# Right-side SBUF tiles moved by 96 bytes, and the second products of a feed-forward block issued output by output

## The chip, the cores and the metric

The kernel runs on one core of one Trainium2 chip. The metric is device time in microseconds (us), the median of several runs. TensorE (PE) multiplies, VectorE (DVE), ScalarE (ACT) and GpSimd (POOL) do the element-wise work, SyncE (SP) issues nearly all transfers.

## What is computed

Causal attention with a decay bias (4 batches, 8 heads, 576 positions, head size 64), then two feed-forward blocks over all 4 x 576 = 2304 tokens, with 64-bit weights, the rest float32:

```python
scores = q @ k.T / 8 + min(-(cum_i - cum_j), 0), causal; attn = softmax(scores); x = attn @ v
h = x @ w_in;  x = max(0.01 * h, h) @ w_out                              # block 0
h = x @ w_in2; out = (max(h, 0) + log1p(exp(-|h|))) @ w_out2             # block 1
```

with `w_in` 512 x 2048 and `w_out` 2048 x 512.

## The kernel before

Every float32 matrix is split into a high part of float32r type and a low part that holds the rest (`xh`/`xl`, `wih`/`wil`, `woh`/`wol`, `gh`/`gl`), and a product is three passes: high with high, high with low, low with high. The first 276 us are attention, with some of block 0 run in between (class `Fill`). The loop from line 685 on does the rest of block 0 and all of block 1.

The 2048 hidden features are cut into 16 tiles of 128, four tiles (`G = 4`) to a weight group, so each block has four groups. The tokens are cut into chunks of 512, 512, 256, 512 and 512 (for the first group of block 0, two chunks of 288). One **step** is one hidden tile `f` of one chunk of one group:

- `h_mm` (line 137) makes the hidden tile: 12 matmuls into one PSUM bank, `xh`, `xl`, `xh` moving, weights `wih`, `wih`, `wil`, four times.
- `act1` (line 599) applies the activation. In block 1 that is a chain over engines: ACT makes `e` and `l`, POOL makes `t` (line 619), DVE makes `gf` (624), ACT makes `gh` (149), POOL makes `gl` (150), one step behind the other.
- `out_mm` (line 632) runs three steps later (`LAG = 3`). It adds the hidden tile's share to the outputs: four outputs in block 0 (rows of the model size, `gh`/`gl` moving, weights `woh`/`wol`), and `N // 128` outputs in block 1 (token tiles, `woh`/`wol` moving 512 columns, `gh`/`gl` as weights). Each output has one PSUM bank (`ps_out`, five buffers) which collects all four steps of a chunk; at the fourth (`f == G - 1`) each output is added into `acc` by DVE (line 662; copied by ACT, line 660, in the first group), and in the last group of block 1 stored (line 665).

The order inside `out_mm` before: first, output by output, the two passes with `gh`; then, output by output, the pass with `gl`; then, after all of it, the sums. All instructions of an engine run in the order of the program; the two planned weight splits (`split_w`) put DVE, ACT and POOL work between the steps.

Pools with `side="right"` are stacked downwards from the end of SBUF. In the built program every tile on the left that TensorE reads (`xh` at byte 16,512 of each partition, `wih` at 90,240, `woh` at 106,624) starts at a multiple of 128, and every tile on the right (the loop's `gh` and `gl` from 212,960 to 227,296, `gf`, `t`, `e`, `l`, and the raw weights and `gh`/`gl` of `Fill`) starts 96 bytes behind one.

Of the kernel before, what the change touches and what calls it, by code (L numbers as in the profile page):

```python
# [9 lines left out]
F32 = mybir.dt.float32  # L10
# [7 lines left out]
P = 128  # L18
NEG = -8.0e9
G = 4  # L20
# [10 lines left out]
def attn_moe_moe(ctx, tc, q, k, v, s, w1i, w1o, w2i, w2o, out):  # L31
    nc = tc.nc
# [7 lines left out]
    NG = NF // G  # L40
# [9 lines left out]
    def pool(name, bufs=1, **kw):  # L50
        return tc.tile_pool(name=name, bufs=bufs, **kw)

    dram = ctx.enter_context(pool("dram", space=bass.MemoryType.DRAM))
    keep = ctx.enter_context(pool("keep"))


    xh = keep.tile([P, KD, NT], F32R, tag="xh", name="xh")
    xl = keep.tile([P, KD, NT], F32R, tag="xl", name="xl")
# [7 lines left out]
    def later(n, fn, *args):  # L66
        todo.setdefault(clock[0] + n, []).append((fn, args))
# [515 lines left out]
    def acc_tile(c, i):  # L583

        c0, N = c
        n = 512 // N
        return acc[:, i * n:(i + 1) * n, c0:c0 + N]
# [42 lines left out]
    outs = {}  # L630

    def out_mm(n):
        layer, g, c, _, _, f = steps[n]
        c0, N = c
        gh, gl = gs.pop(n)
        wh, wl = wt[layer, g * G + f, "o"]
        n_out = KD if layer == 0 else N // P

        for i in range(n_out):
            if f == 0:  # L640
                outs[i] = ps_o.tile([P, 512], F32, tag="o", name="ps_out")
        for low in range(2):
            for i in range(n_out):
                sl = slice(i * P, (i + 1) * P)
                if layer == 0:
                    ps, ops = outs[i][:, :N], ((wh[:, sl], gh), (wl[:, sl], gh), (wh[:, sl], gl))
                else:
                    ps, ops = outs[i], ((gh[:, sl], wh), (gh[:, sl], wl), (gl[:, sl], wh))
                for m, (a, b) in enumerate(ops):
                    if (m == 2) == low:  # L650
                        nc.tensor.matmul(ps, a, b, start=f == 0 and m == 0, stop=f == G - 1 and m == 2)  # L651
        if f < G - 1:
            return
        for i in range(n_out):
            if layer == 0:
                d, o = acc[:, i, c0:c0 + N], outs[i][:, :N]
            else:
                d, o = acc_tile(c, i), outs[i].rearrange("p (a x) -> p a x", x=N)
            if g == 0:
                nc.scalar.activation(d, o, AF.Copy)  # L660
            else:
                nc.vector.tensor_tensor(d, o, d, op=ALU.add)  # L662
            if layer == 1 and g == NG - 1:
                r = c0 + i * P
                nc.sync.dma_start(out[r:r + P, :].rearrange("p (a x) -> p a x", x=N), d)
        if layer == 0 and g == NG - 1:
            later(1, split_x, slice(c0, c0 + N))


# [1 line left out]
    start = {}  # L671
    for n, st in enumerate(steps):
        start.setdefault(st[:2], n)
    for gi, (layer, g) in enumerate(groups[1:]):
        a, z = start[groups[gi]], start[layer, g]
        when = [a + 2, a + 5, a + 8, a + 11, z - 3, z, z - 1, z + 2]
        for j, n in enumerate(when):
            if gi == 0 and j < 4:
                continue
            f, nm = divmod(j, 2)  # L680
# [4 lines left out]
    for n, (layer, g, c, is_first, is_last, f) in enumerate(steps):  # L685
        N = c[1]
        cols = slice(c[0], c[0] + N)
        ps = ps_h.tile([P, 512], F32, tag="h", name="ps_h")
        h_mm(ps[:, :N], layer, g * G + f, xh[:, :, cols], xl[:, :, cols])
        tick()  # L690
        act1(n, layer, N, ps)
        for fn, w in sorted(plan.pop(n, ()), key=lambda x: x[0] is load_w):
            fn(*w)
        if n >= LAG:
            out_mm(n - LAG)
    for n in range(len(steps) - LAG, len(steps)):
        tick()
        out_mm(n)
# [48 lines left out]
```

## Time and profile before

| what | before |
|---|---|
| median of 3 runs | 1022.04 us (1021.41 to 1022.06) |
| span of the profiled execution, first to last instruction | 1020.2 us |
| instructions | 15105 |
| PE busy | 992.0 us, 97% |
| POOL, ACT, DVE busy | 559.2, 536.8, 506.3 us |
| mean granted TensorE clock | 0.997 |

The profiled execution's own time is its span plus what lies around it: the median of the runs is 1.8 us above the span. Matmuls are pipelined, so a matmul's listed duration (some 0.39 us for 512 columns) overlaps the next one's; the pace is the distance from start to start, which the chain of waits (pieces of 12 matmuls) and the timeline show. On the timeline a piece "x4" is four instructions that follow each other, and a bracket names the idle time before an instruction and what ended it. Time stretches: attention to 276 us, block 0 to about 600 us, block 1 to the end.

### The profile page before, as it was taken

The numbers are of one execution on the slowest core, as the hardware profiler recorded it, in microseconds if no ns is written. First come the engines' busy times: TensorE is split into PE (matmuls) and PEld (weight loads), VectorE is DVE, ScalarE is ACT, GpSimd is POOL, SyncE is SP. The second block draws the span as 40 slices with busy tenths as digits, with TensorE's granted clock in tenths as the row PEclk, the third lists the DMA queues.
The fourth block names the chain that finished last, engine by engine and source line by source line (L and its number), as shares of the span: only waits on it lengthen the run. The fifth ranks groups of instructions, "written<-read, shape, count | busy, mean of one in ns | idle before, by whom it ended". The sixth has DMA issues, their size and how long they took to land.

```text
span 1020.2 us, 15105 instructions
## 1 busy us (share of the span) xinstructions
PE 992.0 (97%) x5498; PEld 812.4 (80%) x5498; DVE 506.3 (50%) x1133; ACT 536.8 (53%) x1152; POOL 559.2 (55%) x565
## 2 busy tenths in 40 slices
PE   7889999999999999999999998999999999999998
PEld 4667788888998888888888887888778877888886
DVE  6886665554021312321244158547575767576443
ACT  4877676656355333432444365666645554565452
POOL 6757455434156335533553356667766676667453
PEclk9999999999999999999999999999999999999999
DMA  5422333210252002100220021101210121010202
GB/s 172 135 97 67 113 106 101 93 59 25 73 205 76 22 1 83 63 21 1 83 62 22 16 68 41 42 2 45 80 42 1 42 82 42 1 42 21 83 22 83
DMA packets 38518, 62.04 MB, mean 61 GB/s; under 512 B 2932, under 2 KB 25972, under 8 KB 38444
## 3 DMA queue, kind: packets, MB, share of 16 engines
q1 hardware_dynamic: 38204, 60.74, 18.2%
q8 instruction: 44, 0.72, 0.3%
q10 hardware_dynamic: 240, 0.33, 0.1%
q14 instruction: 30, 0.25, 0.1%
HBM read 52.65 MB, written 8.40 MB: 60 GB/s over the span
## 4 chain that ended last, share of the span: by engine, by line
PE 73%; POOL 10%; DVE 8%; issue 6%; ACT 3%; DMA 0%; DVEq 0%; POOLq 0%; ACTq 0%
PE ps_h L143 30%; PE ps_out L651 27%; PE pt_v L354 4%; PE ps_o L539 4%; PE pt_s L262 4%; POOL t L619 3%; PE pt_t L323 3%; POOL gl L150 2%; POOL wm L120 2%; DVE wm L114 2%; PE pt_s L252 2%; ACT sc L295 1%; DVE wm L111 1%; DVE wm L117 1%; POOL wil L130 1%
## 5 line engine op out<-in xcount | busy, mean ns | idle before, releaser
L150 POOL TENSOR_TENSOR gl<-gf,gh 128x512 fp32r<-128x512 f32 (+2 forms) x148 | 178.3, 1206 | 258.9 <-ACT gh L149 243.4
L143 PE MATMUL ps_h<-xh,wih 128*128 128x512 f32 (+2 forms) x688 | 246.5, 358 | 1.1 <-ACT o L543 0.6
L143 PE MATMUL ps_h<-xl,wih 128*128 128x512 f32 (+2 forms) x688 | 244.7, 356 | 0.0
L143 PE MATMUL ps_h<-xh,wil 128*128 128x512 f32 (+2 forms) x688 | 243.9, 354 | 0.0
L143 PEld LDWEIGHTS ps_h<-xh,wih 128*128 128x128 f32 x688 | 129.4, 188 | 21.5 <-ACT o L543 0.8
L306 POOL TENSOR_SCALAR sc<-sc,st 128x512 f32<-128x512 f32 (+4 forms) x160 | 88.1, 562 | 103.8 <-DVE st L302 61.3
L143 PEld LDWEIGHTS ps_h<-xl,wih 128*128 128x128 f32 x688 | 129.4, 188 | 19.0
L143 PEld LDWEIGHTS ps_h<-xh,wil 128*128 128x128 f32 x688 | 129.4, 188 | 18.5
L662 DVE TENSOR_TENSOR acc<-ps_out,acc 128x512 f32<-128x512 f32 (+1 forms) x114 | 67.7, 655 | 129.1 <-PE ps_out L651 129.1
L149 ACT ACTIVATE gh<-gf 128x512 fp32r<-128x512 f32 (+2 forms) x148 | 85.3, 576 | 82.7 <-DVE gf L624 81.8
L605 ACT ACTIVATE gf<-ps_h 128x512 f32<-128x512 f32 (+2 forms) x68 | 36.7, 539 | 172.1 <-PE ps_h L143 168.2
L651 PE MATMUL ps_out<-woh,gh 128*128 128x512 f32 x288 | 116.2, 403 | 5.8 <-ACT gh L149 3.2
L624 DVE TENSOR_TENSOR gf<-gf,t 128x512 f32<-128x512 f32 (+1 forms) x80 | 56.0, 700 | 127.0 <-POOL t L619 127.0
L111 DVE TENSOR_SCALAR wm<-wm 128x512 f32<-128x512 f32 x64 | 42.1, 658 | 147.3 <-ACT wm L105 140.3
L651 PE MATMUL ps_out<-wol,gh 128*128 128x512 f32 x288 | 115.0, 399 | 0.0
L295 ACT ACTIVATE sc<-sc,st 128x512 f32<-128x512 f32 (+2 forms) x144 | 83.3, 581 | 42.9 <-DVE st L286 22.0
L120 POOL TENSOR_TENSOR wm<-wm,wt 128x512 int32<-128x512 int32 x64 | 88.1, 1377 | 28.0 <-DVE wm L117 28.0
L619 POOL TENSOR_TENSOR t<-e,t 128x512 f32<-128x512 f32 (+1 forms) x80 | 98.3, 1228 | 0.0
L651 PE MATMUL ps_out<-gh,woh 128*128 128x512 f32 (+2 forms) x272 | 97.1, 365 | 0.0
L651 PE MATMUL ps_out<-gh,wol 128*128 128x512 f32 (+2 forms) x272 | 96.6, 364 | 0.0
L281 DVE CUSTOM_DVE_ANT_0 sc<-pt_s,mask 128x512 f32<-128x512 f32 (+2 forms) x144 | 66.7, 480 | 57.2 <-PE pt_t L323 46.1
L651 PE MATMUL ps_out<-woh,gl 128*128 128x512 f32 x288 | 80.6, 397 | 1.2 <-POOL gl L150 1.1
(93 smaller groups left out, 1729.2 us busy)
## 6 DMA issues: line engine op xcount, KB each, us to landing
rawi<-in_moe_w_in SPq DMA_DIRECT2D x32, 512.0 KB
rawo<-in_moe_w_out SPq DMA_DIRECT2D x32, 512.0 KB
V<-in_v SPq DMA_DIRECT2D x16, 320.0 KB
Q<-in_q SPq DMA_DIRECT2D x15, 320.0 KB
K<-in_k SPq DMA_DIRECT2D x16, 288.0 KB
out<-acc SPq DMA_DIRECT2D x18, 256.0 KB
part<-o SPq DMA_DIRECT2D x24, 144.0 KB
acc<-part SPq DMA_DIRECT2D x6, 576.0 KB
```

The source lines that it names most:

```text
L111: nc.vector.tensor_scalar(mf, mf, D_MIN, D_MAX, op0=ALU.max, op1=ALU.min)
L120: nc.gpsimd.tensor_tensor(m, m, t, op=ALU.add)
L143: nc.tensor.matmul(ps, a, b, start=n == 0, stop=n == 3 * KD - 1)
L149: nc.scalar.activation(gh, gf, AF.Copy)
L150: nc.gpsimd.tensor_tensor(gl, gf, gh.bitcast(F32), op=ALU.subtract)
L281: nc.vector.tensor_tensor_reduce(out=self.sc[:, j, c], in0=self.ps[j][:, c], in1=m, scale=-scale, scalar=3.0e38, op0=ALU.add, op1=ALU.min, ...
L295: nc.scalar.activation(x, x, AF.Exp, scale=-1.0, bias=self.stat(0, e), accum_out=self.stat(1, e))
L306: nc.gpsimd.tensor_scalar(x, x, self.stat(2, e), 1.0, op0=ALU.mult, op1=ALU.mult)
L619: nc.gpsimd.tensor_tensor(t, e, t, op=ALU.subtract)
L624: nc.vector.tensor_tensor(gf, gf, t, op=ALU.add)
L651: nc.tensor.matmul(ps, a, b, start=f == 0 and m == 0, stop=f == G - 1 and m == 2)
L662: nc.vector.tensor_tensor(d, o, d, op=ALU.add)
```

## The change

A pool of 96 bytes per partition is opened first on the right side and keeps its place to the end, and `out_mm` is rewritten:

```diff
-
+    edge = ctx.enter_context(pool("edge", side="right"))
+    edge.tile([P, 24], F32, tag="edge", name="edge")
...
-        for low in range(2):
-            for i in range(n_out):
...
-                for m, (a, b) in enumerate(ops):
-                    if (m == 2) == low:
-                        nc.tensor.matmul(ps, a, b, start=f == 0 and m == 0, stop=f == G - 1 and m == 2)
-        if f < G - 1:
-            return
         for i in range(n_out):
+            sl = slice(i * P, (i + 1) * P)
...
+            for m, (a, b) in enumerate(ops):
+                nc.tensor.matmul(ps, a, b, start=f == 0 and m == 0, stop=f == G - 1 and m == 2)
+            if f < G - 1:
+                continue
             if layer == 0:
                 d, o = acc[:, i, c0:c0 + N], outs[i][:, :N]
```

Every right-side tile starts 96 bytes lower in the built program, `gh` and `gl` at 212,864 to 227,200: multiples of 128, as on the left. The left side stays. Nothing writes or reads the new tile.

Each output's three passes now stand together, and on the last step of a chunk its sum follows in the program. The number of instructions is the same on every engine, and their order differs on PE alone: the sums were already the next instructions of DVE (or ACT), and stay where they were; what they wait for on PE comes earlier.

PE, one step of block 0 in the middle of a chunk (`ps_out` numbers are PSUM tiles), before and with the change:

```order
L651 MATMUL ps_out_4876<-gh_4825,woh_4318 128x512 [waits Activation_49]
L651 MATMUL ps_out_4876<-gh_4825,wol_4320 128x512
L651 MATMUL ps_out_4877<-gh_4825,woh_4318 128x512
L651 MATMUL ps_out_4877<-gh_4825,wol_4320 128x512
L651 MATMUL ps_out_4878<-gh_4825,woh_4318 128x512
L651 MATMUL ps_out_4878<-gh_4825,wol_4320 128x512
L651 MATMUL ps_out_4879<-gh_4825,woh_4318 128x512
L651 MATMUL ps_out_4879<-gh_4825,wol_4320 128x512
L651 MATMUL ps_out_4876<-gl_4826,woh_4318 128x512 [waits Pool_49]
L651 MATMUL ps_out_4877<-gl_4826,woh_4318 128x512
L651 MATMUL ps_out_4878<-gl_4826,woh_4318 128x512
L651 MATMUL ps_out_4879<-gl_4826,woh_4318 128x512
```

```order
L650 MATMUL ps_out_4880<-gh_4829,woh_4322 128x512 [waits Activation_49]
L650 MATMUL ps_out_4880<-gh_4829,wol_4324 128x512
L650 MATMUL ps_out_4880<-gl_4830,woh_4322 128x512 [waits Pool_49]
L650 MATMUL ps_out_4881<-gh_4829,woh_4322 128x512
L650 MATMUL ps_out_4881<-gh_4829,wol_4324 128x512
L650 MATMUL ps_out_4881<-gl_4830,woh_4322 128x512
L650 MATMUL ps_out_4882<-gh_4829,woh_4322 128x512
L650 MATMUL ps_out_4882<-gh_4829,wol_4324 128x512
L650 MATMUL ps_out_4882<-gl_4830,woh_4322 128x512
L650 MATMUL ps_out_4883<-gh_4829,woh_4322 128x512
L650 MATMUL ps_out_4883<-gh_4829,wol_4324 128x512
L650 MATMUL ps_out_4883<-gl_4830,woh_4322 128x512
```

The wait for POOL's `gl` moves from the ninth matmul to the third, and the bank changes four times in a step where it changed eight times.

PE, the first step of the last chunk of block 1, where the banks must be free of the chunk before, before and with the change:

```order
L651 MATMUL ps_out_9754<-woh_8349,gh_9692 128x512 [waits PE_49,Activation_49]
L651 MATMUL ps_out_9754<-wol_8351,gh_9692 128x512
L651 MATMUL ps_out_9755<-woh_8349,gh_9692 128x512 [waits DVE_49]
L651 MATMUL ps_out_9755<-wol_8351,gh_9692 128x512
L651 MATMUL ps_out_9756<-woh_8349,gh_9692 128x512 [waits DVE_49]
L651 MATMUL ps_out_9756<-wol_8351,gh_9692 128x512
L651 MATMUL ps_out_9757<-woh_8349,gh_9692 128x512 [waits DVE_49]
L651 MATMUL ps_out_9757<-wol_8351,gh_9692 128x512
L651 MATMUL ps_out_9754<-woh_8349,gl_9693 128x512 [waits Pool_49]
```

```order
L650 MATMUL ps_out_9758<-woh_8353,gh_9696 128x512 [waits PE_49,Activation_49]
L650 MATMUL ps_out_9758<-wol_8355,gh_9696 128x512
L650 MATMUL ps_out_9758<-woh_8353,gl_9697 128x512 [waits Pool_49]
L650 MATMUL ps_out_9759<-woh_8353,gh_9696 128x512 [waits DVE_49]
L650 MATMUL ps_out_9759<-wol_8355,gh_9696 128x512
L650 MATMUL ps_out_9759<-woh_8353,gl_9697 128x512
L650 MATMUL ps_out_9760<-woh_8353,gh_9696 128x512 [waits DVE_49]
L650 MATMUL ps_out_9760<-wol_8355,gh_9696 128x512
L650 MATMUL ps_out_9760<-woh_8353,gl_9697 128x512
L650 MATMUL ps_out_9761<-woh_8353,gh_9696 128x512 [waits DVE_49]
```

The waits for DVE's sums of the chunk before move from the third, fifth and seventh matmul to the fourth, seventh and tenth.

## Rows read from the trace of the kernel before

**Rows 1.** The page, part 1: busy time of each engine, share, instructions.

```profile
PE 992.0 (97%) x5498; PEld 812.4 (80%) x5498; DVE 506.3 (50%) x1133; ACT 536.8 (53%) x1152; POOL 559.2 (55%) x565
```

**Rows 2.** The chain in order of time (start, us, what): 512 columns in block 0.

```profile
527.73 2.76 PE ps_h L143 x12
530.49 2.81 PE ps_out L651 x12
```

**Rows 3.** The same chain, block 1: 512 columns, and a step with two outputs.

```profile
906.53 2.73 PE ps_h L143 x12
909.26 2.81 PE ps_out L651 x12
...
973.23 1.40 PE ps_out L651 x6
```

**Rows 4.** Timeline of PE, block 1: one `h_mm`, its fourth matmul and its twelfth.

```profile
907.06 0.39 PE L143 MATMUL ps_h<-xh,wih 128*128 128x512 f32 x1
...
908.87 0.39 PE L143 MATMUL ps_h<-xh,wil 128*128 128x512 f32 x1
```

**Rows 5.** Timeline of PE, block 0: a step's first matmul, its four with gl, what follows.

```profile
469.02 0.40 PE L651 MATMUL ps_out<-gh,woh 128*128 128x512 f32 x1
...
470.90 1.10 PE L651 MATMUL ps_out<-gl,woh 128*128 128x512 f32 x4
471.83 0.40 PE L143 MATMUL ps_h<-xh,wih 128*128 128x512 f32 x1
```

**Rows 6.** Timeline of PE: a step of 256 columns in block 0, and what follows.

```profile
460.61 0.28 PE L651 MATMUL ps_out<-gh,woh 128*128 128x256 f32 x1
...
462.05 0.39 PE L143 MATMUL ps_h<-xh,wih 128*128 128x512 f32 x1
```

**Rows 7.** The chain in order of time: an `h_mm` of 256 columns in block 0.

```profile
543.09 1.44 PE ps_h L143 x12
```

**Rows 8.** Groups by line and form: first passes of block 0 and block 1.

```profile
L651 PE MATMUL ps_out<-woh,gh 128*128 128x512 f32 x288 | 116.2, 403 | 5.8 <-ACT gh L149 3.2 <-DVE acc L662 2.1 <-ACT acc L660 0.5
L651 PE MATMUL ps_out<-gh,woh 128*128 128x512 f32 x192 | 76.3, 398 | 0.0
```

**Rows 9.** Busy time by stretch: length, PE, PEld, DVE, ACT, POOL, granted clock, DMA.

```profile
697.00:766.00 69.00, 66.79 (x308) 53.77 (x307) 48.24 (x64) 40.38 (x75) 49.25 (x39) 1.00 0.14 46
800.00:867.00 67.00, 64.92 (x300) 52.40 (x299) 50.90 (x69) 36.90 (x67) 46.76 (x36) 1.00 0.15 48
```

**Rows 10.** Timeline, block 1, 761 to 763 us: a step with two outputs.

```profile
761.25 0.40 PE L651 MATMUL ps_out<-woh,gh 128*128 128x512 f32 x1
...
761.65 0.72 POOL L150 TENSOR_TENSOR gl<-gf,gh 128x256 fp32r<-128x256 f32 x1
...
762.43 0.73 PE L651 MATMUL ps_out<-woh,gl 128*128 128x512 f32 x2 [0.55 <-POOL gl L150]
```

**Rows 11.** Timeline, block 1, 833 to 847 us: a late `gl`, then a wait for sums.

```profile
833.96 0.40 PE L651 MATMUL ps_out<-woh,gh 128*128 128x512 f32 x1
...
834.27 1.29 POOL L150 TENSOR_TENSOR gl<-gf,gh 128x512 fp32r<-128x512 f32 x1
...
835.61 1.20 PE L651 MATMUL ps_out<-woh,gl 128*128 128x512 f32 x4
...
846.69 0.50 PE L651 MATMUL ps_out<-woh,gh 128*128 128x512 f32 x1 [1.12 <-DVE acc L662]
```

**Rows 12.** Timeline of the last step, 1008 to 1017 us.

```profile
1008.08 1.28 POOL L150 TENSOR_TENSOR gl<-gf,gh 128x512 fp32r<-128x512 f32 x1 [1.47 <-ACT gh L149]
...
1012.06 0.50 PE L651 MATMUL ps_out<-woh,gh 128*128 128x512 f32 x1
1012.08 1.29 POOL L150 TENSOR_TENSOR gl<-gf,gh 128x512 fp32r<-128x512 f32 x1 [1.47 <-ACT gh L149]
...
1014.04 1.10 PE L651 MATMUL ps_out<-woh,gl 128*128 128x512 f32 x4
1014.47 2.48 DVE L662 TENSOR_TENSOR acc<-ps_out,acc 128x512 f32<-128x512 f32 x4 [3.13 <-PE ps_out L651]
```

More of the change, by code (lines that the diff above doesn't have):

```diff
@@ L641, in out_mm @@
                 outs[i] = ps_o.tile([P, 512], F32, tag="o", name="ps_out")
-        for low in range(2):
-            for i in range(n_out):
[L644 to L648, printed above, removed]
-                for m, (a, b) in enumerate(ops):
-                    if (m == 2) == low:
-                        nc.tensor.matmul(ps, a, b, start=f == 0 and m == 0, stop=f == G - 1 and m == 2)
-        if f < G - 1:
-            return
-        for i in range(n_out):
+        for i in range(n_out):
+            sl = slice(i * P, (i + 1) * P)
+            if layer == 0:
+                ps, ops = outs[i][:, :N], ((wh[:, sl], gh), (wl[:, sl], gh), (wh[:, sl], gl))
+            else:
+                ps, ops = outs[i], ((gh[:, sl], wh), (gh[:, sl], wl), (gl[:, sl], wh))
+            for m, (a, b) in enumerate(ops):
+                nc.tensor.matmul(ps, a, b, start=f == 0 and m == 0, stop=f == G - 1 and m == 2)
+            if f < G - 1:
+                continue
             if layer == 0:
@@ L665, in out_mm @@
                 nc.sync.dma_start(out[r:r + P, :].rearrange("p (a x) -> p a x", x=N), d)
-        if layer == 0 and g == NG - 1:
+        if layer == 0 and g == NG - 1 and f == G - 1:
             later(1, split_x, slice(c0, c0 + N))
```

## The prediction

> **What bounds the kernel now.** Read the busy times first: PE is busy 97% of the span [rows 1], and the other engines at most 55%. A busy PE can still be slow, so read next the pace in the chain of waits, which follows PE in pieces of 12 matmuls, one `h_mm` and one `out_mm` in turn. In block 0 twelve matmuls of 512 columns take 2.76 us in `h_mm` and 2.81 us in `out_mm` [rows 2]; in block 1 it is 2.73 and 2.81 [rows 3]. They have the same shape and type. Within an `h_mm` the settled pace is (908.87 - 907.06) / 8 = 0.2263 us for each matmul [rows 4], 2.716 for twelve. So an `out_mm` of 512 columns runs 2.81 - 2.716 = 0.094 us behind what the same engine does with other operands, some 0.008 per matmul, and an `h_mm` behind one in block 0 is still 0.03 slower than in block 1.
>
> What differs in `out_mm`? Three things, and the change touches each. (a) The bank: an `out_mm` changes its output bank eight times, an `h_mm` once. But in one step the eight matmuls of the first part, with four changes of bank, take (470.90 - 469.02) / 8 = 0.235 us each, and the four with `gl`, which change it every time, (471.83 - 470.90) / 4 = 0.2325 [rows 5]. Twice the changes, and no slower. (b) The place: `gh` or `gl` is an operand of every `out_mm` matmul (moving in block 0, weights in block 1) and starts 96 bytes behind a multiple of 128; all operands of `h_mm` start at one. (c) The sequence of operands. Against (b) stands one row: with 256 columns of `gh` moving, `out_mm` takes (462.05 - 460.61) / 12 = 0.120 us per matmul [rows 6], and `h_mm` with 256 columns 1.44 / 12 = 0.120 [rows 7]. If the place costs, it does so only where 512 columns move.
>
> **The change, part by part.**
>
> *The 96 bytes.* It moves every right-side tile onto the 128-byte grid and adds no work. How often the slow pace occurs: 192 first passes with `gh` moving 512 columns are 192 / 4 = 48 steps of block 0; 288 in block 1 are 64 steps with four outputs (256) and 16 with two (32) [rows 8]. If place is the cause, these steps come down to 0.2263 per matmul: 48 x 0.094 = 4.5 us, 64 x 0.094 = 6.0, and 16 x (1.40 - 6 x 0.2263 = 0.042) = 0.7 [rows 3, 4]. The `h_mm` of block 0 follow with 2.76 - 2.73 = 0.03 each, 48 x 0.03 = 1.4 [rows 2, 3]. Sum 12.6. Bounds: 12.6 at best, zero if the place doesn't matter; a loss I leave out of the range, since in `h_mm` both operands start at such multiples and that is the best pace of the trace. I take 12.6, because both kinds of `out_mm` with 512 columns have a right-side operand and are slow, and `h_mm`, which has none, settles at the fast pace.
>
> By the Trainium skill ("SBUF — State Buffer", sections "Specifications (TRN2)" and "Operand start alignment") SBUF is read in lines of 16 bytes, and a start address has only to be a multiple of the element's size. Both 96 behind a multiple of 128 and the multiple itself start a 16-byte line, so by that rule this term would be 0 instead of 12.6; the page says that its measurements of start addresses timed nothing, and it names no coarser step. Rows of 256 columns agree with it, those of 512 columns are not told by it. It is the first rival below.
>
> *Three passes together.* Same matmuls, same weight loads, fewer changes of bank. By (a) a change of bank costs nothing that the rows show; the bounds are 0 and half of the 11.2 of `out_mm` (four changes in place of eight), 5.6. I take 0, which the two paces of [rows 5] are nearest to.
>
> *The earlier need of `gl`.* PE now reads `gl` with the third matmul. In block 0 the lead is several us and nothing happens. In block 1 POOL makes `gl` in the chain `t`, `gf`, `gh`, `gl`, one per 1012.08 - 1008.08 = 4.0 us when nothing else is planned [rows 12], and with the weight splits it falls behind twice in the middle groups. PE's order is fixed, so behind a waiting matmul stand the rest of the step and the next `h_mm`.
> At 762 us the matmul with `gl` waits now, until 762.43; two matmuls are left behind it [rows 10]. Afterwards four are left: the step ends 2 x 0.234 = 0.47 later. The same place comes once more, at 866. Two times: +0.9.
> At 834 `gl` ends at 834.27 + 1.29 = 835.56, while the third matmul stands at 833.96: a wait of 1.6 us, and ten matmuls behind it in place of four, so the step ends 6 x 0.234 = 1.4 later. But two steps on PE waited 1.12 us for sums of DVE anyway [rows 11], which come when DVE's planned work lets them, and their need moves back from the third matmul to the fourth, 0.23 more; that takes 1.35 of the 1.4. I cost it at 0; without that cover it is 1.4. The same pair of places stands once before, near 731 and 743.
>
> *Earlier sums.* DVE's order stays. In the middle of the kernel the sums wait for DVE's turn, so I cost this at 0. At the end it counts: now the four sums start with the ninth matmul's end, at 1014.47, and last 2.48, to 1016.95 [rows 12]. Afterwards `gl` is there at 1012.08 + 1.29 = 1013.37, ten matmuls remain, the last starts at about 1013.43 + 9 x 0.234 = 1015.54, ends 0.40 later, and one sum of 2.48 / 4 = 0.62 follows: 1016.56. That is 0.4 sooner; without the wait for `gl` it would be more.
>
> *What the cover takes back.* Where POOL's chain sets the end of a stretch, a faster PE only waits longer. These are 697 to 762 us and 800 to 866, the stretches in which PE is idle 2.2 and 2.1 us [rows 9], and the last three steps. A step of 2.73 + 2.81 = 5.54 us gains 0.094, or 1.7%: 131 x 1.7% = 2.2, and 3 x 0.094 = 0.3 at the end. Together 2.5 given back.
>
> **Sum.** -12.6 + 2.5 + 0.9 - 0.4 = -9.6. The profiled span is 1020.2 and would be 1010.6; the runs' median is 1.8 above the span, so 1022.0 - 9.6 = **1012.4 us**.
>
> **The rivals.**
>
> 1. *The place does not matter* (chance 0.24). For it: 256 columns from the right side run at the pace of the left [rows 6, 7]. Against it: 512 columns don't [rows 2, 3]. Then only the order is left: +0.9 - 0.4 = +0.5, 1022.5 us, no change.
> 2. *Part of the excess goes* (0.17): the bank, the sequence of operands or the place each carry a share, for instance half. -6.3 + 1.3 + 0.5 = -4.5: 1017.5 us. For it: the slow pace reaches into the following `h_mm` of block 0, so it is no fixed price of one operand. Against: [rows 5] shows no bank price.
> 3. *The waits for `gl` are paid in full, and the pace stays* (0.09). PE's order is fixed; if the element-wise chain in turn waits for PE's next `h_mm`, nothing absorbs. The two places shown cost 1.6 and 762.37 - 761.25 = 1.1 (`gl` ends 0.72 behind 761.65 [rows 10]), each twice: 5.4, less 0.4 at the end: 1027.0, slower. Against it: `out_mm` runs three steps behind `h_mm`, so the chain's next input is made before the wait, and the wait for sums at 846.69 takes up what came late [rows 11]. It makes the kernel slower by over 2.0 us only if the pace gains less than 5.4 - 0.4 - 2.0 = 3.0; with the whole gain of 12.6 the kernel is faster even so.
>
> **How the numbers follow.** A measurement of this kernel can tell about 0.2%, 2.0 us, from no change. My forecast, that the 512-column excess goes nearly whole, has a chance of 0.50 and its own range is 1009.5 to 1015.5: below it nothing is given back (1022.0 - 12.6 = 1009.4), above it rival 2 begins. The range for 8 in 10 reaches from 1009.5 over rival 2 to rival 1 with its half us of doubt, 1023.0; what is left out is rival 3 and little below. Faster: 0.50 + 0.17 = 0.67. Same: 0.24. Slower: 0.09.
>
> **What would show it.** In the chain of the changed kernel, pieces of 12 `ps_out` matmuls at 2.72 to 2.74 us in both blocks and pieces of `ps_h` in block 0 at 2.73: place (or sequence) was the cause. Pieces still at 2.81: rival 1. PE's waits for POOL `gl` should rise from two to eight or more, with the largest near 731 and 834, while the waits there for DVE's sums shrink. The first sum of the last step should start some 0.4 us behind the start of its third matmul, and the last should end about 0.6 us behind the end of the last matmul. I am wrong if `ps_out` pieces are at 2.72 and the time has still not fallen: then the chain over POOL sets far more of block 1 than the two stretches.

## The result, and the profile after

The changed kernel takes 1011.0 us (median of 4 runs, 1010.34 to 1011.55) against 1021.72 for the kernel before, run beside it (1021.19 to 1022.06): a ratio of 0.9895, with a 95% interval of 0.9882 to 0.9908. It is faster by 10.7 us, where 9.6 was forecast.

The page of the changed kernel, span and part 1, which answers to [rows 1]:

```profile
span 1008.5 us, 15105 instructions
...
PE 979.3 (97%) x5498; PEld 811.6 (80%) x5498; DVE 516.5 (51%) x1133; ACT 536.3 (53%) x1152; POOL 558.8 (55%) x565
```

The same instructions, and PE is busy 12.7 us less with them. DVE's busy time has grown by 10 us with the same 1133 instructions; it is not the bound at 51%.

The chain in order of time (start, us, what), block 0 and then block 1, the answer to [rows 2, 3]:

```profile
525.43 2.72 PE ps_out L650 x12
528.15 2.72 PE ps_h L144 x12
...
895.12 2.72 PE ps_out L650 x12
897.84 2.72 PE ps_h L144 x12
```

All four kinds of piece have become one: 2.72 us, where 2.76, 2.81, 2.73 and 2.81 stood. `h_mm`, whose text didn't change, has become faster with `out_mm`.

PE's waits in the loop (us in total, times, longest) of the changed kernel:

```profile
PE ps_out L650 <- POOL gl L151: 6.9, 8, 1.9
...
PE ps_out L650 <- ACT gh L150: 1.9, 2, 1.7
...
PE ps_out L650 <- ACT acc L658: 0.4, 1, 0.4
```

and of the kernel before:

```profile
PE ps_out L651 <- ACT gh L149: 3.2, 3, 2.6
PE ps_out L651 <- DVE acc L662: 2.1, 2, 1.1
...
PE ps_out L651 <- POOL gl L150: 1.1, 2, 0.6
```

The two waits for `gl` have become eight, those for DVE's sums are gone. Busy time in the two stretches that answer to [rows 9] (the columns are the same):

```profile
690.00:756.00 66.00, 62.62 (x294) 51.27 (x293) 47.76 (x62) 37.58 (x71) 46.76 (x37) 1.00 0.15 48
793.00:860.00 67.00, 64.47 (x298) 53.45 (x297) 50.07 (x66) 37.09 (x69) 47.24 (x38) 0.97 0.15 48
```

PE is idle 3.4 and 2.5 us there (66.00 - 62.62, 67.00 - 64.47), where it was 2.2 and 2.1.

The step that was at 833.96 before [rows 11], on the timeline of the changed kernel:

```profile
825.77 1.26 POOL L151 TENSOR_TENSOR gl<-gf,gh 128x512 fp32r<-128x512 f32 x1
...
827.08 0.50 PE L650 MATMUL ps_out<-woh,gl 128*128 128x512 f32 x1 [1.91 <-POOL gl L151]
...
828.50 0.63 PE L650 MATMUL ps_out<-wol,gh 128*128 128x512 f32 x1
828.93 0.63 PE L650 MATMUL ps_out<-woh,gl 128*128 128x512 f32 x1
...
831.49 0.43 PE L144 MATMUL ps_h<-xh,wil 128*128 128x512 f32 x1
```

This is the largest of the eight waits for `gl`, and the matmul behind it does wait with the rest of its step. Some 1 us behind the wait the matmuls begin to stand 0.43 us apart: the lower of the clock's two levels, 1.2 GHz, for some 3 us. The granted clock from 828.5 to 831.5 us is 0.50, and 0.97 over the whole stretch.

The end, to be held against [rows 12]:

```profile
1002.16 0.51 PE L650 MATMUL ps_out<-woh,gl 128*128 128x512 f32 x1
...
1002.70 2.79 DVE L660 TENSOR_TENSOR acc<-ps_out,acc 128x512 f32<-128x512 f32 x4 [2.63 <-PE ps_out L650]
...
1004.37 0.40 PE L650 MATMUL ps_out<-woh,gl 128*128 128x512 f32 x1
```

The first sum starts 0.54 us behind the start of the third matmul, and the last ends (1002.70 + 2.79 = 1005.49) 0.72 behind the end of the last matmul, 1004.77.

**Where the time went** is read from the start of `out_mm`s that are easy to find again. Between two `h_mm` stands one run of `ps_out` matmuls; counted from 0 (the first at about 282 us), run 68 is near the change of blocks, 77, 97 and 117 enclose the two stretches in which POOL is late, 140 is near the end. The table has the distances from start to start in the timelines, in us, one profiled execution each, and the last line the whole from run 0 to the end of the span. Attention ahead of run 0 is left out: its code is the same everywhere, and run 0 starts between 281.33 and 282.80.

| runs | before | place alone (1) | order alone (2) | the change | before, no `t` (7) | place, no `t` (8) |
|---|---|---|---|---|---|---|
| 0 to 68 | 331.87 | 326.20 | 331.87 | 326.20 | 331.87 | 326.20 |
| 68 to 77 | 48.06 | 48.09 | 47.29 | 47.08 | 45.11 | 46.36 |
| 77 to 97 | 103.46 | 102.94 | 103.62 | 103.17 | 99.92 | 98.32 |
| 97 to 117 | 103.30 | 102.78 | 103.52 | 103.06 | 99.92 | 98.32 |
| 117 to 140 | 112.30 | 110.56 | 112.30 | 110.55 | 112.30 | 110.56 |
| 140 to end | 38.87 | 38.49 | 37.35 | 36.97 | 38.63 | 37.88 |
| all | 737.86 | 729.06 | 735.95 | 727.03 | 727.75 | 717.64 |

The numbers in brackets are the experiments below.

### The profile page after: what moved, and what is told of

Same layout as the page of the kernel before. It is cut to its first block, busy times and chain, and to the rows that moved or that the text cites. A ratio compares the mean times of both kernels' runs of the same rounds, so it can differ in the third digit from the quotient of the medians.

```text
span 1008.5 us, 15105 instructions
## 1 busy us (share of the span) xinstructions
PE 979.3 (97%) x5498; PEld 811.6 (80%) x5498; DVE 516.5 (51%) x1133; ACT 536.3 (53%) x1152; POOL 558.8 (55%) x565
## 4 chain that ended last, share of the span: by engine, by line
PE 69%; POOL 10%; DVE 8%; issue 8%; ACT 3%; DMA 1%; SPq 0%; POOLq 0%; ACTq 0%; DVEq 0%
PE ps_h L144 29%; PE ps_out L650 25%; PE pt_v L355 4%; PE ps_o L540 4%; POOL t L620 3%; PE pt_s L263 3%; PE pt_t L324 3%; POOL gl L151 3%; POOL wm L121 2%; DVE wm L115 2%; PE pt_s L253 1%; DVE wm L118 1%; ACT sc L296 1%; DVE wm L112 1%; DVE sc L282 1%
## 5 line engine op out<-in xcount | busy, mean ns | idle before, releaser
L660 DVE TENSOR_TENSOR acc<-ps_out,acc 128x512 f32<-128x512 f32 (+1 forms) x114 | 72.5, 660 | 99.4 <-PE ps_out L650 99.4
L650 PE MATMUL ps_out<-woh,gl 128*128 128x512 f32 x288 | 113.6, 394 | 7.1 <-POOL gl L151 6.9
L650 PE MATMUL ps_out<-woh,gh 128*128 128x512 f32 x288 | 113.1, 393 | 2.4 <-ACT gh L150 1.9
L650 PE MATMUL ps_out<-wol,gh 128*128 128x512 f32 x288 | 112.8, 392 | 0.0
L650 PE MATMUL ps_out<-gl,woh 128*128 128x512 f32 (+2 forms) x272 | 97.7, 359 | 0.0
```

## The experiments

The theory: the place of the right-side tiles carries the gain, by way of the pace of matmuls with 512 columns moving. The rivals: the order carries it (fewer changes of bank, another sequence of operands), or each has a share. A second question is what about the place matters: the start on a grid of 128 bytes, or something between the two operands. The third is what the waits on POOL take back.

**1. The place alone.** The kernel before with the 96 bytes:

```diff
+    edge = ctx.enter_context(pool("edge", side="right"))
+    edge.tile([P, 24], F32, tag="edge", name="edge")
```

> Only the 96 bytes; the order of the passes and sums as before. Theory P (the start of the right-side operands sets the pace): pieces of 12 second products at 2.72 to 2.74 us in both blocks, time at 1009 to 1011.5 us, the same as with the whole change or up to 1.5 us better, since no wait for gl is moved forward. Theory O (the sequence of operands or the change of banks sets the pace): pieces stay at 2.81 us, time 1021 to 1023 us.

Measured: 1012.65 us, ratio 0.9907 (0.989 to 0.9923). The chain in order of time, block 0 and block 1:

```profile
525.61 2.72 PE ps_out L652 x12
528.33 2.72 PE ps_h L144 x12
...
771.27 2.72 PE ps_out L652 x12
773.99 2.72 PE ps_h L144 x12
```

The place alone brings the whole new pace, in the old order and with eight changes of bank in each step. The time is 1.1 us above the expected range, and not better than the whole change: by the table, place alone lacks the 2.0 us that the order brings (729.06 - 727.03).

**2. The order alone.** The changed kernel without the 96 bytes:

```diff
-    edge = ctx.enter_context(pool("edge", side="right"))
-    edge.tile([P, 24], F32, tag="edge", name="edge")
```

> Only the order: three passes of one output together, sums behind them; right-side tiles 96 bytes past a multiple of 128 as before. Theory P: pieces of 12 second products stay at 2.79 to 2.81 us, time 1021 to 1024 us (the earlier need of gl costs 0 to 2 us). Theory O: pieces at 2.72 us and time at 1009 to 1013 us. A share for each would give pieces between, 2.76 us, and some 1016 us.

Measured: 1019.42 us, ratio 0.9976 (0.9966 to 0.9986): a small gain, where a loss of half a us was forecast. The chain, block 0 and block 1:

```profile
521.94 2.76 PE ps_h L143 x12
524.70 2.81 PE ps_out L649 x12
...
897.58 2.81 PE ps_out L649 x12
900.39 2.73 PE ps_h L143 x12
```

The pace is that of [rows 2, 3]: neither the bank nor the sequence of operands matters to it. So the gain has another source. The table puts it in two places, 0.77 us between runs 68 and 77 and 1.52 behind run 140, and takes 0.16 and 0.22 back in the stretches of the late `gl`. Timeline of the kernel before at these two places:

```profile
610.94 2.49 DVE L662 TENSOR_TENSOR acc<-ps_out,acc 128x512 f32<-128x512 f32 x4 [3.88 <-PE ps_out L651]
613.34 0.68 DVE L624 TENSOR_TENSOR gf<-gf,t 128x512 f32<-128x512 f32 x1
...
626.61 0.68 DVE L624 TENSOR_TENSOR gf<-gf,t 128x512 f32<-128x512 f32 x1
628.01 0.75 PE L651 MATMUL ps_out<-woh,gh 128*128 128x512 f32 x1 [2.57 <-ACT gh L149]
...
657.83 2.04 ACT L660 ACTIVATE acc<-ps_out 128x512 f32<-128x512 f32 x4
...
1000.24 2.48 DVE L662 TENSOR_TENSOR acc<-ps_out,acc 128x512 f32<-128x512 f32 x4 [4.93 <-PE ps_out L651]
1002.64 0.68 DVE L624 TENSOR_TENSOR gf<-gf,t 128x512 f32<-128x512 f32 x1
```

and of the order alone:

```profile
609.31 2.80 DVE L659 TENSOR_TENSOR acc<-ps_out,acc 128x512 f32<-128x512 f32 x4 [2.47 <-PE ps_out L649]
612.03 0.68 DVE L624 TENSOR_TENSOR gf<-gf,t 128x512 f32<-128x512 f32 x1
...
625.31 0.68 DVE L624 TENSOR_TENSOR gf<-gf,t 128x512 f32<-128x512 f32 x1
626.71 0.50 PE L649 MATMUL ps_out<-woh,gh 128*128 128x512 f32 x1 [1.48 <-ACT gh L149]
...
656.51 2.04 ACT L657 ACTIVATE acc<-ps_out 128x512 f32<-128x512 f32 x4
...
998.24 2.80 DVE L659 TENSOR_TENSOR acc<-ps_out,acc 128x512 f32<-128x512 f32 x4 [3.53 <-PE ps_out L649]
1000.95 0.68 DVE L624 TENSOR_TENSOR gf<-gf,t 128x512 f32<-128x512 f32 x1
```

In both places DVE stands idle until the last pass of an output is done, and behind the four sums, in DVE's order, stands the `gf` of a later step, which ACT's `gh`, POOL's `gl` and in the end PE wait for. At the first place the `gf` that PE's wait at 628.01 hangs on is the one at 626.61; weight splits and `xl` stand between, which DVE does almost without a pause. The sums start with the third matmul in place of the ninth. Counted from the start of run 68 or run 140 of the same execution (614.20 and 981.32 before, 613.99 and 980.72 with the order alone), the `gf` behind the sums comes 1.1 us sooner in both places, and the steps behind it follow.

From the `gf` at 626.61 on, the chain over DVE, POOL and ACT takes the same time at both paces of PE. To ACT's copies of the sums (`acc`), which PE waits for at run 76 in the kernel before, it is 657.83 - 626.61 = 31.2 us there, 656.51 - 625.31 = 31.2 with the order alone, 651.52 - 620.30 = 31.2 with the place alone and 650.24 - 619.01 = 31.2 with the change. So between runs 68 and 77 a faster PE mostly waits longer, and an earlier `gf` counts.

**3 and 4. Other places.** The changed kernel with 32 bytes in place of 96 (right-side tiles 64 behind a multiple of 128), and with 64 (32 behind one):

```diff
-    edge.tile([P, 24], F32, tag="edge", name="edge")
+    edge.tile([P, 8], F32, tag="edge", name="edge")
```

```diff
-    edge.tile([P, 24], F32, tag="edge", name="edge")
+    edge.tile([P, 16], F32, tag="edge", name="edge")
```

> The whole change, but with a tile of 32 bytes in place of 96: right-side tiles start 64 bytes past a multiple of 128, so on the 64-byte grid and off the 128-byte grid. Theory P with a grid of 64 bytes: pieces at 2.72 us, time 1010 to 1012 us. Theory P with a grid of 128 bytes: pieces near 2.81 us, time 1021 to 1024 us. Theory O: 2.72 us, 1010 to 1013 us.

> The whole change, but with a tile of 64 bytes: right-side tiles start 32 bytes past a multiple of 128, off the 64-byte grid as before but on the other side of it. Theory P: pieces near 2.81 us, time 1021 to 1024 us, whichever the grid. Theory O, or a price of the distance moved alone: 2.72 us, 1010 to 1013 us.

Measured: 1017.67 us, ratio 0.9956 (0.9941 to 0.9971), and 1018.91, ratio 0.9969 (0.9957 to 0.9981). The chain at 64 bytes behind a multiple, block 0 and block 1:

```profile
525.08 2.77 PE ps_h L144 x12
527.85 2.76 PE ps_out L650 x12
...
905.68 2.80 PE ps_out L650 x12
908.48 2.75 PE ps_h L144 x12
```

The chain at 32 bytes behind one, block 1:

```profile
893.87 2.73 PE ps_h L144 x12
896.60 2.79 PE ps_out L650 x12
```

The `out_mm` of neither comes to 2.72, and both times hold the gain of the order besides (1.9 us in the table). A grid of 64 or 32 bytes isn't it; at 64 the excess of block 0's `out_mm` over 2.72 is halved (0.04 in place of 0.09), that of block 1's hardly changed.

**5. All operands 96 bytes behind a multiple of 128.** The kernel before, with the 96 bytes opened first on the left, so that `xh`, the weights and all else there move to where the right side already stands:

```diff
+    keep.tile([P, 24], F32, tag="edge", name="edge")
```

> The kernel before, with a tile of 96 bytes first on the LEFT side: now every tile that TensorE reads, left and right, starts 96 bytes past a multiple of 128, and moving operand and weights have the same distance from the grid. Theory A (each operand's own start against a 128-byte grid costs): second products stay at 2.81 us or more and first products of 512 columns rise from 2.73 to 2.76 to about 2.80 to 2.90 us; time 1027 to 1045 us. Theory B (the distance between the starts of the moving operand and the weights costs): all pieces at 2.72 us, time 1010 to 1014 us.

Measured: 1013.71 us, ratio 0.9916 (0.9901 to 0.9931). The chain, block 0 and block 1:

```profile
526.68 2.72 PE ps_out L651 x12
529.40 2.72 PE ps_h L143 x12
...
902.36 2.72 PE ps_out L651 x12
905.08 2.72 PE ps_h L143 x12
```

No operand of the loop starts at a multiple of 128 now, and the pace is the best one. It isn't the start on the grid that matters; that both operands start at the same remainder fits, and experiment 9 tries it from the other side.

**6. Sums output by output only where there are sums.** The changed kernel, with the old order in the three steps of four that have none, so that `gl` is needed late there:

```diff
+        if f < G - 1:
+            for i in range(n_out):
+                passes(i, (0, 1))
+            for i in range(n_out):
+                passes(i, (2,))
+            return
+        for i in range(n_out):
+            passes(i, (0, 1, 2))
```

> The whole change, but only the fourth step of a chunk goes output by output with its sums behind them; the three other steps keep the pass with gl last. The place stays at 96 bytes, so pieces at 2.72 us. If the late gl in steps that carry no sum costs something at the end of the chains, 1 to 2 us under the whole change (1009 to 1010.5 us). If those waits are taken up by the next wait anyway, the same 1010.5 to 1011.5 us.

Measured: 1009.85 us (1009.53 to 1010.96), ratio 0.9884 (0.9869 to 0.9898). It clearly beats the kernel before; against the change (0.9882 to 0.9908) the intervals overlap, so a gain over it isn't shown. From run 0 to the end it takes 1008.96 - 282.74 = 726.22 us, 0.8 less than the change.

**7 and 8. Without POOL's `t`.** Two kernels that leave out the subtraction that gives the small correction of `log1p` in block 1, so that POOL has one instruction less of about 1.3 us in each step: the kernel before, and the same with the 96 bytes.

```diff
-        nc.gpsimd.tensor_tensor(t, e, t, op=ALU.subtract)
```

> The kernel before without POOL's instruction t<-e,t of block 1 (the small correction of log1p is left out, its sum on DVE stays): POOL's chain is 1.3 us shorter per step, so PE's waits for gh, gl and sums in block 1, 12 us, should mostly go: 1010 to 1016 us, pieces at 2.81 us as before. Only meaningful against e8.

> e7 with the 96 bytes on the right side. Theory G (part of the pace gain is given back where POOL's chain sets the end): with the chain out of the way the 96 bytes bring the full 12 to 13 us against e7. Rival (the pace gain itself is only about 9.4 us, nothing is given back): 9 to 10 us against e7, as e1 against before.

Measured: 1011.86 us, ratio 0.9903 (0.9886 to 0.9919), and 1002.01, ratio 0.9805 (0.9791 to 0.982). The 12 us of waits in the first expectation are too many: the kernel before lists 6.9 in the loop (3.2 + 2.1 + 1.1, and 0.5 for ACT's copies). Without `t` the loop is 10.1 us shorter (737.86 - 727.75). PE's one remaining wait of the loop in each of the two, first in the kernel before without `t`:

```profile
PE ps_out L650 <- ACT gh L149: 1.6, 1, 1.6
```

and with the place as well:

```profile
PE ps_out L651 <- ACT gh L150: 1.9, 1, 1.9
```

The difference of the two times alone, 9.85 us, is what the rival named (nothing given back); the stretches of the table decide. With POOL out of the way, the place is worth 1.60 us in each of the stretches 77 to 97 and 97 to 117; with POOL's chain in place it is 0.52 (table). The 1.08 that each gives back is what the waits take. The last three steps give back 0.75 - 0.38 = 0.37. From run 0 to the end the place gains 727.75 - 717.64 = 10.1 us without `t`. In the second of the two kernels the matmuls behind the wait stood 0.43 us apart (granted clock 0.54 from 622.7 to 626.4), so that the step of run 70 took 626.36 - 621.91 = 4.45 us where experiment 1, behind its wait of 2.8, needed 624.56 - 621.70 = 2.86, and experiment 7 2.89. Without these 1.6 the gain is 11.7, against 8.8 with POOL's chain (737.86 - 729.06): 2.9 given back.

**9. Different remainders, on the left.** The kernel before, with 96 bytes behind `xl`: `xh` and `xl` stay at a multiple of 128, the weights move to 96 behind one, where `gh` and `gl` are. So `out_mm` gets equal remainders and `h_mm` different ones.

```diff
     xl = keep.tile([P, KD, NT], F32R, tag="xl", name="xl")
+    keep.tile([P, 24], F32, tag="edge", name="edge")
```

> The kernel before, with a tile of 96 bytes on the left side right behind xh and xl: these stay on the 128-byte grid, and everything else that TensorE reads (wih, woh, the attention's tiles, gh, gl) starts 96 bytes past it. Theory B (the distance between the moving operand's start and the weights' start): the second products, where both are at 96, fall to 2.72 us, and the first products of 512 columns, where xh is at 0 and wih at 96, rise to 2.79 to 2.81 us in both blocks; 128 - 16 = 112 slow first products of twelve in place of 112 slow second ones, so the time comes out near the kernel before, 1019 to 1025 us. Rival (the right side or the sequence of gh and gl costs, whatever the distance): first products stay at 2.72 to 2.76 us, time 1010 to 1014 us.

Measured: 1021.18 us, ratio 0.9993 (0.9983 to 1.0002): no change. But the chain, block 0 and block 1, has turned round:

```profile
526.45 2.81 PE ps_h L144 x12
529.25 2.73 PE ps_out L652 x12
...
902.67 2.73 PE ps_out L652 x12
905.40 2.81 PE ps_h L144 x12
```

`h_mm` has taken on the slow pace and `out_mm` lost it. So the cost follows the pair of operands, wherever they lie, left or right, and the sequence of `gh` and `gl` or the right side as such is excluded.

The paces together (us for twelve matmuls with 512 columns moving, by the remainders modulo 128 of the moving operand and the weights, in whichever order):

| remainders | distance | 12 matmuls | seen in |
|---|---|---|---|
| 0 and 0, everywhere | 0 | 2.72 | the change, 1, 8 |
| 96 and 96, everywhere | 0 | 2.72 | 5 |
| 0 and 0, or 96 and 96, next to slow ones | 0 | 2.73 to 2.77 | `h_mm` before, 2 to 4; `out_mm` of 9 |
| 0 and 96 | 96 | 2.81 | `out_mm` before, 2; `h_mm` of 9 |
| 0 and 64 | 64 | 2.76 (block 0), 2.80 (block 1) | `out_mm` of 3 |
| 0 and 32 | 32 | 2.80, 2.79 | `out_mm` of 4 |

## Why the prediction was right, and where it wasn't

- **The pace (12.6).** Right: the pieces of `ps_out` are at 2.72, and place alone does it (experiments 1 and 2). Without POOL's cover it came to 11.7 (experiments 7 and 8), and 5.67 of the 5.9 forecast for block 0 are on the table's first line. The argument "both kinds of `out_mm` with 512 columns have a right-side operand and are slow, and `h_mm`, which has none, settles at the fast pace" held. What I called its cause, a start off the 128-byte grid, was too narrow: experiment 5 is off the grid with everything, and fast. What counts is whether the moving operand and the weights start at the same remainder modulo 128 (experiments 5 and 9); the best pace of the trace had been read from the one pair that did, and a zero remainder was taken for the reason. For this change the two readings give the same number. By the rule of the Trainium skill ("SBUF — State Buffer", sections "Specifications (TRN2)" and "Operand start alignment") that SBUF is read in lines of 16 bytes, the term would have been 0. Experiment 1 differs from that: the measurement decides.
- **Three passes together (0).** Right: experiment 2 has four changes of bank in a step in place of eight, and the old paces.
- **The earlier need of `gl` (+0.9).** The waits went from two to eight, as forecast, with the largest in the loop's later groups at 827 and the next at 724, the places of 834 and 731; but the two stretches cost only 0.23 and 0.28 us more than with the place alone, 0.5 in all (0.4 in experiment 2). The cover named for 834, the wait for DVE's sums, did what the working says: 1.91 us of waiting for `gl` in the change, and no wait for sums after it, against 0.64 and then 1.26 us for sums in experiment 1. That the lower clock would follow the wait (1.4 us, below) stood in no term of the forecast.
- **"In the middle of the kernel the sums wait for DVE's turn, so I cost this at 0."** Wrong near the change of blocks. Where DVE is idle ahead of the sums (3.88 us in the row at 610.94), their earlier start passes on to `gf` behind them and to `gh`; 1.0 us between runs 68 and 77 (48.09 - 47.08), 0.77 in experiment 2, where PE, after a wait for `gl` and the lower clock at run 70, reaches run 76 so late that it has no wait there.
- **The end (-0.4).** Too small: 1.52 in both pairs of the table. I worked out the last step alone and didn't see that the group of sums at 1000.24 stands ahead of a `gf` on DVE in the same way, so that the steps after it start sooner too, by 1.1 us (experiment 2). The last step itself came out as forecast: from the start of its `gl` to the end of the span it takes 1020.19 - 1012.08 = 8.11 us in the kernel before and 1018.07 - 1010.40 = 7.67 with the order alone, 0.44 less. The two estimates of the last step itself (first sum 0.4 behind the third matmul's start, last sum 0.6 behind the last matmul's end) came out at 0.54 and 0.72.
- **Given back (2.5).** Right: 2.9, of it 1.08 in each stretch (2.2 forecast for the two), 0.37 in the last three steps (0.3 forecast), and some 0.4 that I hadn't seen, between runs 68 and 77, where the chain of 31.2 us sets the time: place alone gains nothing there. It waits 2.8 us for `gh`, and then 0.65 for `gh` and 0.92 for ACT's copies at run 76. There the kernel before, whose step of run 70 took 632.46 - 628.01 = 4.45 us at the lower clock against 2.86, waits only 0.17, and the two are level again.
- **The sum.** Forecast -12.6 + 2.5 + 0.9 - 0.4 = -9.6; by the table -11.7 + 2.9 + 0.5 - 1.5 - 1.0 = -10.8, which is 727.03 - 737.86. The order, taken for a loss of 0.5, is a gain of 2.0, clear of no change in experiment 2; the place, pace gain less what is given back, brought 8.8 where 10.1 was forecast. These two misses go opposite ways, so it is partly luck that the time came so near. Rival 1 (place does nothing) is excluded by experiment 1, rival 3 (waits paid in full) by the table, rival 2 (half) by the pieces at 2.72.

Open: why rows of 256 and 288 columns don't show the cost in any of these kernels, why 64 bytes cost less than 32 or 96 in block 0 but not in block 1, and what in the chip makes a difference of the two starts count. A matmul's moving operand was compared with its own weights; whether the weights loaded beside it for the next matmul are the partner that counts, these runs can't tell, since within a slow piece both start at the same remainder. No run looked into the engine.

## What to carry to other kernels

Look at the pace of matmuls of one shape across the program, not only at the busy share: a piece of twelve that takes 2.81 us where another takes 2.72 is a question, at 97% busy too. If the two operands come from different stacks of tiles, compare their start addresses modulo 128, and shift one stack so that they agree; that costs a few bytes and no instruction. It is shown here for float32r with 512 columns, for starts that differ by 32, 64 or 96; with 256 and 288 columns it made no difference. Where a sum or another small piece of work stands on an in-order engine ahead of the chain that PE will wait for, and the engine is idle before it, an earlier start passes on to that chain: 1.1 us at each of two places here. And where such a chain sets the time, what PE gains or loses within it is taken up by its next wait.

## What the runs showed of the hardware

- A matmul of float32r with 512 columns moving goes at 0.2267 us (2.72 / 12) when moving operand and weights start at the same remainder modulo 128 (0 or 96 were tried), and at up to 0.234 when they don't, slower by 3%. It reaches into neighbours with equal remainders (2.76 for `h_mm` beside 2.81 for `out_mm` [rows 2]).
- The lower level of the clock came behind some waits and not behind others, and not by their length: behind 2.57 us in the kernel before and 1.91 in the change the matmuls stood 0.43 us apart for some 3 us, behind 2.82 in experiment 1 they didn't, behind 2.83 in experiment 5 they did for 2 us. In the change this cost (831.49 - 828.50) - 7 x 0.2267 = 1.4 us at that place. Little of it was left later: counted from run 0 of each, the change is 0.77 us ahead of experiment 1, which had none of it, at run 110 (543.10, 543.87), 0.17 behind at run 113 (561.95, 561.78), and ahead by 0.50 again at 117 (579.51, 580.01).
- The idle time that is listed for a wait isn't its whole price: from run 77 to 97 the kernel before lists four waits of PE with 0.37 + 0.95 + 0.34 + 0.55 = 2.21 us, and without POOL's `t`, where it has none of them, the stretch is 103.46 - 99.92 = 3.54 us shorter, some 0.3 more for each wait.
